# Gated FFT filter and state-space mix: x loaded by halves of its row groups, turned copies on VectorE, transform results on ScalarE

## The chip, the cores and the metric

The kernel runs on one core of one Trainium2 chip. The metric is the device time of one execution in microseconds (us), as the median of several runs. Five engines matter: TensorE (PE; its weight loads are listed apart as PEld), VectorE (DVE), ScalarE (ACT), GpSimd (POOL) and SyncE (SP), which here only issues DMA transfers. Matmul results are written to PSUM, everything else on the chip lies in SBUF, both with 128 partitions.

## The reference: what is computed

x has S = 2048 tokens of D = 1024 channels in bf16. The output mixes two branches of x by one gate per token:

```
g = sigmoid((x * gate_w).sum(-1))
a = irfft2(rfft2(x) * (w_r + 1j * w_i))            # over tokens and channels
h[t] = Lam_bar * h[t-1] + (B_bar @ x[t])           # complex, 1024 states
b = 2 * real(C @ h[t]) + x * Dskip
out = g * a + (1 - g) * b
```

The two-dimensional transform and its inverse are done as matmuls with tables of cosines and sines; the recurrence is done on VectorE with scans, between a multiplication by B on TensorE and one by C on TensorE.

## The kernel before: how it is tiled, staged and ordered

**Layout of x.** Partition p first holds the 16 tokens 16p to 16p+15, so "row" j of the text is the group of 128 tokens 16p + j. Rows 0 to 11 are loaded in natural layout into tiles called CT by SP (`load_x`, L242): one transfer for row 0, one for row 1, then five for two rows each (512 KB). TensorE then turns each of these rows, which means 8 transposes of 128x128 into one PSUM tile `pt` (`turn`, L919), and ScalarE copies the turned row into xQ, in which channels lie on partitions and tokens along the free axis (`turn_out`, L929). The source is read with a step there: order (c q g) in PSUM becomes (c, g, j, q) in xQ, so neighbouring elements of the source go to two halves g. Rows 12 to 15 come through two transposing DMA transfers (L238) into CT and are copied by ScalarE from SBUF to xQ (L925).

**The transform.** `fold` on VectorE (L943 to L954) makes sums and differences of channel halves of the turned rows: one row at a time for rows 0 to 3, two at a time for rows 4 to 15. The `fd` matmuls (L430 to L443) transform along channels into PSUM `ps_fd`; `fd_out` (L449) copies these to the tiles X, on VectorE for the groups listed in `FD_DVE` and on ScalarE for the others. The `s1` matmuls (L462) do the first step along tokens into `ps_s`; `s1_out` (L474) copies these to CT or A tiles, on VectorE for the groups listed in `S1_DVE`. SP stores them to a scratch in memory (L480), from which later stages load them.

**The recurrence.** SP loads the B matrices by 16 transposing DMA transfers (`load_B`, L259) into BT. `unit_mm` (L398) multiplies 256 columns of xQ, taken over all 16 turned rows, by BT into `psu`; so the first unit matmul needs every copy into xQ. `unit_out` (L408) copies the result to h, and VectorE multiplies by tables (`make_tab`, L281 to L307) and scans (L347 to L378). The matmuls by C (L713), the inverse transform (L594 to L671, L810) and the last matmuls (L727) follow on TensorE, and the outputs are mixed and stored.

**What sets the order.** No scheduler is at work: within one engine instructions run in program order, and the program order is written by hand. `ORDER` is a string of about 1,000 letters, one for each step of one generator: x is a step of `load_x`, T of `turn`, U of `turn_out`, f of `fold`, F of the fd matmuls and E of their copies, S of the s1 matmuls and A of their copies, G and 2 of the loads of the tables, b of `load_B`, h of `unit_mm` and H of its copies, v of the recurrence, whose pieces are numbered in `PIECES`. `SLOTS` says which of four PSUM slots each PSUM tile takes. `FILL_T` puts 22 idle transposes ahead of row 2, where TensorE would stand still otherwise. In xQ, j is a row, c a chunk of tokens, g the half and q the place in the chunk.

Of the kernel before, what the change touches and what calls it, by code (L numbers as in the profile page):

```python
# [26 lines left out]
NCH = S // TC  # L27
# [5 lines left out]
NTURN = 12  # L33
# [1 line left out]
FILL_V = (0, 0, 4)  # L35
FILL_T = {2: 22}
WARM = 7
FD_DVE = (2, 4, 6, 7)
CAST_ACT = (5, 6, 7)
ANG_ACT = (4, 5, 6, 7)  # L40
CARRY_POOL = ()
S1_DVE = (1, 4, 5)
CLOSES = (0, 1, 2, 3, 10, 4, 5, 11, 12, 6, 7, 8, 9)
PIECES = (
# [6 lines left out]
)  # L51
SLOTS = (
    "0123012310231023102310230123012031201312031203101230132031231031201312303312013213021021013010320130",
    "1220123203201320130130120321023120320321021023120312301230231201302303120",
)
MIRROR = (6, 7, 8, 9)
ORDER = (
    "xxxTVUVVVaTfVVrrUGTGG|Tfaaa|UafFffftafftUftxFEfTETUFffU22xSEkSTSTArxAfffUAUFTTEUfffUFbxwxbxbbTUEFbfE",
    "1bT~SSUfuFSFAUUUU2bbtbfAF1AtbbtrFttrbEffE11EbEh11SStbttfttttAg1~HtfufhA~tetFSSFrKHrtu1EAvfAEhtttvttt",
    "SSFtbbvvvAtEttH1Avthtftv1cttwv1tcthccctttvtcch~HFtvftHvvhuHtvfStEettStAHhtAeKrvFctcvvFhEEHKtvwtcSvtS",  # L60
    "hvvKc1vcc1vAAKKvv1c1v1hcvswcsLMvvveHHekMYsssnNHvvhHnsvvvJWWMvs3vsvNvvsssssnvssnvvs4NMvv4Njvhv553vhvv",
    "YvyJJL46H4vv5WWvhh5vvvMM78Jj7HHmn3nHvv8M44m6MnN77WW5jv+Yy5vvv3M845+mNY8nMJJMyvvv+467hvHMh5vN7N34vHmh",
    "4J8m+6n3h8v77HmH+55v4n64JMvNnMYy5vW83n+v7N474vJ568vYmmNJ7dh7NWj+v58v5vyvvd88MhvHHm8+MJm6h+n378vv7Hh8",
    "J+d4Y4YX5vv5NnJH6XXv7ny7mNNm8+hn8hvqivvvvvJvqyHihYivvyiqhivqqiYvNImvni+qJJmHIIiini+HinvdIIH+vvIIIqIN",
    "IiiiNmI+vvIInvvImvyJqii%NJINIJYJYmhvvv+vvvlylzvhHmplpzZZH+mZZZhlZvhPPRR++zyRRRlQDQHzRZZmRHZ+ZRZvoOZD",
    "QvlpDzzPovOvQBvZZlpPYvZZvBZDZRDRRRvzQDoloOBzoQOopZOoPOBlzlZRoDDZZvBZZRpQvzCvYZZvZZBZZPRDoQoo9RQQ9yRR",
    "0RRyCooD099C9Y990DD0D0Y00",
)

EVEN = ((0, 0), (2, 1), (2, 0), (0, 1))  # L70
# [72 lines left out]
def kernel(  # L143
# [17 lines left out]
    nc = tc.nc  # L161
    x = A_x[0]
# [57 lines left out]
    x_gjq = xQ.rearrange("p c d (g j q) -> p c d g j q", g=2, j=16)  # L220
# [2 lines left out]
    tab = tabp.tile([P, 4, 8, TC], BF16, name="tab")  # L223

    xn = [CT[i // 4][:, 2 * (i % 4):2 * (i % 4) + 2, :] for i in range(8)]
    x_v = x.rearrange("(p j) d -> p j d", j=16)
    x_sg = x.rearrange("(s g j) d -> g s (j d)", g=2, j=16)
    xt = CT[1][:, 4:8].rearrange("p a k -> p (a k)").rearrange("p (j d g s) -> p j d g s", j=4, d=8, g=2)
    fft = {}
# [4 lines left out]
    def load_x():  # L234
        for i in range(8):
            if i >= NTURN // 2:
                g = i - NTURN // 2
                nc.sync.dma_start_transpose(out=xt[:, :, :, g].rearrange("p j d s -> p (j d) s"), in_=x_sg[g][:, NTURN * D:])  # L238
                yield
                continue  # L240
            for js in (slice(0, 1), slice(1, 2)) if i == 0 else (slice(0, 2),):
                nc.sync.dma_start(out=xn[i][:, js], in_=x_v[:, 2 * i + js.start:2 * i + js.stop, :])  # L242
                yield

    def load_T2():
# [200 lines left out]
    def fd_out():  # L446
        for j in range(16):
            X1 = X1s[j] = gta.tile([P, 2, K], BF16, name="X1", bufs=4)
            (nc.vector.tensor_copy if j in FD_DVE else nc.scalar.copy)(  # L449
                out=X1.rearrange("p r (m e c) -> p r m e c", e=2, c=2),  # L450
# [15 lines left out]
    def s1_out():  # L466
        for j in range(16):
# [4 lines left out]
            else:  # L472
                A1 = tmp.tile([P, 2, K], BF16, name="A1_last", tag=("ang", "rot_kk", "sn_f", "cs_f")[j - 12])
            (nc.vector.tensor_copy if j in S1_DVE else nc.scalar.copy)(out=A1, in_=pss.pop(j))  # L474
            A1s[j] = A1
# [435 lines left out]
    pts = {}  # L911
# [9 lines left out]

    def turn_out():
        for j in range(16):
            if j >= NTURN:
                nc.scalar.copy(out=x_gjq[:, :, :, :, j, :].rearrange("p c d g q -> p d g c q"),  # L925
                               in_=xt[:, j - NTURN].rearrange("p d g (c q) -> p d g c q", c=NCH))
                yield
                continue
            nc.scalar.copy(out=x_gjq[:, :, :, :, j, :].rearrange("p c d g q -> p d c g q"),  # L929
                           in_=pts.pop(j).rearrange("p d (c q g) -> p d c g q", c=NCH, g=2))  # L930
            yield

    def fold():
# [228 lines left out]
    def once(f):  # L1162
# [3 lines left out]
    late_tiles = tuple(range(NEARLY))  # L1166
    acts = {
        "V": turn_vectors(), "|": turn_late_vectors(), "T": turn(), "U": turn_out(), "f": fold(), "~": mirror(), "u": fold_odd(), "F": fd(), "E": fd_out(), "S": s1(), "A": s1_out(), "1": s1_store(),
        "K": keep_A1(), "h": unit_mm(), "H": unit_out(), "t": chain(*(make_tab(jp) for jp in range(4))), "r": radii(), "a": small(),
        "g": once(gate), "e": gate_out(), "b": load_B(), "c": load_C(), "2": load_T2(), "x": load_x(), "G": load_G(), "w": load_Wcols(), "k": load_turns(),  # L1170
        "n": early_mm(), "N": early_out(), "J": early_store(), "s": middle(), "L": load_small(), "M": load_mid(), "W": load_W(),
        "3": s2(), "4": s2_out(), "j": unit_cols(), "5": times_w(), "6": is1(), "7": is1_out(), "8": is1_store(), "q": load_last(), "i": is2(), "I": is2_out(),
# [43 lines left out]
```

## Time and profile before

| what | value |
|---|---|
| median of 3 runs | 306.29 us (305.23, 306.57, 306.29) |
| span of the profiled execution, first to last instruction | 303.6 us |
| median less that span, which lies around it | 2.69 us |
| busy PE, DVE, ACT, POOL | 296.4, 289.3, 188.5, 73.3 us |
| granted TensorE clock | full in every slice |
| mean traffic with memory | 166 GB/s over the span |

The profiled execution has no time of its own beside the runs, so its span is set against the median: what lies outside the span is taken as the same before and after. A start in the timeline is in us from the start of the span; the difference of two starts on one busy engine is what one instruction really occupies, which is a little less than the duration printed for it, since instructions on VectorE and ScalarE overlap by about 0.1 us.

### The profile page before, as it was taken

Reading aid. Unit: us, or ns where it says so; the run is one execution under the profiler, and the core shown is the slowest. Engines: PE = TensorE matmul, PEld = TensorE weight load, DVE = VectorE, ACT = ScalarE, POOL = GpSimd, SP = SyncE. Lnnn points to the kernel's source line nnn. Section 1 sums busy time; section 2 is a strip of 40 time slices with the busy share of each in tenths; the row PEclk is TensorE's granted clock in tenths of the full one; section 3 lists DMA queues with packets and bytes.
Section 4 is the critical chain, followed back from the end, with each engine's and each line's share of the span. In section 5 each row is a group of like instructions: output and inputs, shape, how many; then the busy total and the mean of one; then the engine's idle time right before and its main releaser. Section 6 shows DMA issues by size and latency. Waiting matters only on the chain. (4 is left out here: it accounts for less than half of the span.)

```text
span 303.6 us, 6402 instructions
## 1 busy us (share of the span) xinstructions
PE 296.4 (98%) x2568; PEld 197.4 (65%) x2592; DVE 289.3 (95%) x340; ACT 188.5 (62%) x255; POOL 73.3 (24%) x99
## 2 busy tenths in 40 slices
PE   8999999999999999999999999999999999999995
PEld 5664677878864685458553866669657986645543
DVE  2999999999999999999999999999899999999995
ACT  4999999896532383667665865529668774343400
POOL 2100420745893001110210220202011253252330
PEclk9999999999999999999999999999999999999999
DMA  6999999989999599895948798687758876978976
GB/s 208 341 201 194 253 193 310 162 142 154 268 214 241 160 259 219 181 250 189 212 96 258 163 223 225 139 294 147 242 174 185 165 88 135 160 132 143 165 153 181
DMA packets 74157, 59.35 MB, mean 196 GB/s; under 512 B 44904, under 2 KB 61680, under 8 KB 74128
## 3 DMA queue, kind: packets, MB, share of 16 engines
q1 hardware_dynamic: 66560, 49.82, 65.8%
q0 software_dynamic: 6912, 8.69, 23.0%
q10 hardware_dynamic: 656, 0.44, 0.5%
q8 instruction: 20, 0.33, 0.4%
q14 instruction: 9, 0.07, 0.1%
HBM read 27.46 MB, written 23.08 MB: 166 GB/s over the span
## 5 line engine op out<-in xcount | busy, mean ns | idle before, releaser
L398 PE MATMUL psu<-xQ,BT 128*128 128x256 bf16 x1024 | 116.5, 273 | 0.2 <-DVE X L449 0.2
L398 PEld LDWEIGHTS <-BT 128*128 128x128 bf16 x1024 | 99.0, 98 | 17.3 <-issue 4.6
L713 PE MATMUL ps_y<-CT,h 128*128 128x512 bf16 x397 | 92.5, 379 | 0.9
L363 DVE TENSOR_TENSOR_SCAN h<-rz,h 128x2048 bf16<-128x2048 f32 (+1 forms) x20 | 70.8, 3561 | 0.0
L713 PEld LDWEIGHTS <-h 128*128 128x128 bf16 x416 | 39.6, 98 | 46.3 <-issue 2.9
L785 POOL DMA_DIRECT2D y_scratch<-su x20 | 17.3, 902 | 135.7 <-ACT su L779 105.4
L408 ACT CAST h<-psu 128x1024 bf16<-128x1024 f32 x32 | 32.3, 1011 | 18.7 <-PE psu L398 13.1
L350 DVE TENSOR_TENSOR h<-h,tab 128x4096 bf16<-128x4096 bf16 (+1 forms) x20 | 37.1, 1859 | 0.1
L744 ACT ACTIVATE ye<-ps_y,omg 128x512 f32<-128x512 f32 x26 | 17.9, 689 | 26.3 <-PE ps_y L713 11.8
L347 DVE TENSOR_TENSOR xQ<-h,tab 128x4096 bf16<-128x4096 bf16 x12 | 27.4, 2284 | 1.0 <-ACT h L408 1.0
L603 ACT CAST X<-ps_s 128x1024 bf16<-128x1024 f32 x16 | 16.2, 1010 | 14.6 <-PE ps_s L594 11.2
L727 PE MATMUL ps_q<-CT,h 128*128 128x512 bf16 (+2 forms) x110 | 21.3, 348 | 0.2
L817 ACT ACTIVATE BT<-ps_id,gB 128x1024 bf16<-128x1024 f32 x14 | 15.3, 1114 | 9.9 <-PE ps_id L810 5.7
L671 ACT CAST ZT<-ps_is 128x1024 bf16<-128x1024 f32 x16 | 15.8, 1017 | 6.2 <-PE ps_is L661 6.2
L637 ACT CAST C<-ps_is 128x1024 bf16<-128x1024 f32 x16 | 15.7, 1011 | 5.1 <-DMA xQ<-in_A_x_dram 3.4
L851 POOL DMA_DIRECT2D BT<-y_scratch x10 | 13.1, 1452 | 19.7 <-DVE BT L846 13.3
L727 PEld LDWEIGHTS <-h 128*128 128x128 bf16 x112 | 10.3, 98 | 10.4 <-DVE h L378 0.5
L779 ACT ACTIVATE su<-xs,omg 128x512 f32<-128x512 bf16 x20 | 14.2, 723 | 4.1 <-DMA y_scratch<-su 2.2
L929 ACT COPY xQ<-pt 128x1024 bf16<-128x1024 bf16 x12 | 12.2, 1082 | 1.3 <-PE pt L919 1.3
L449 ACT CAST X<-ps_fd 128x1024 bf16<-128x1024 f32 x12 | 12.3, 1062 | 1.0 <-PE ps_fd L439 0.9
L617 DVE TENSOR_TENSOR UV<-X,Wb 128x2048 bf16<-128x2048 bf16 x8 | 9.6, 1220 | 0.6 <-ACT ye L744 0.6
L617 DVE TENSOR_TENSOR UV<-X,raw 128x2048 bf16<-128x2048 bf16 x8 | 9.8, 1223 | 0.2 <-ACT X L604 0.2
(200 smaller groups left out, 397.3 us busy)
## 6 DMA issues: line engine op xcount, KB each, us to landing
y_scratch<-ye SPq DMA_DIRECT2D x20, 256.0 KB, 4.6
y_scratch<-su POOLq DMA_DIRECT2D x20, 256.0 KB, 4.7
Bb<-turn_scratch SPq DMA_DIRECT2D x16, 256.0 KB, 5.2
turn_scratch<-C SPq DMA_DIRECT2D x16, 256.0 KB, 4.1
raw<-turn_scratch SPq DMA_DIRECT2D x8, 512.0 KB, 4.3
xs<-in_A_x_dram SPq DMA_DIRECT2D x13, 256.0 KB, 3.9
out_dram<-BT SPq DMA_DIRECT2D x11, 256.0 KB, 4.3
CT<-in_A_x_dram SPq DMA_DIRECT2D x5, 512.0 KB, 6.1
```

Of the source, the lines that this page charges most:

```text
L347: nc.vector.tensor_mul(out=tmps["s"], in0=u[:, ::-1], in1=bc(i))
L350: nc.vector.tensor_mul(out=u, in0=u, in1=bc(i))
L363: nc.vector.tensor_tensor_scan(out=seg, data0=rz[:, js.start + j:js.start + j + m].rearrange("p j t -> p (j t)"), data1=seg, initial=0.0, ...
L398: nc.tensor.matmul(psu[:, j, :], lhsT=BT[4 * q + j][:, ri, d8, :], rhs=xQ[:, c, d8, :], start=(d8 == 0), stop=(d8 == 7))
L408: nc.scalar.copy(out=hs[c][:, ri, 4 * q:4 * q + 4].rearrange("p b (q j) -> p b q j", j=32), in_=psus.pop((c, q, ri)).rearrange("p b (j q) ...
L603: nc.scalar.copy(out=X2, in_=ps2s[g][b])
L617: nc.vector.tensor_mul(out=UV, in0=X2s.pop((g, b)).unsqueeze(1).to_broadcast([P, 2, 2, K]), in1=fft["Wb"][g // 2 % 2][:, :, at:at + 1, :]. ...
L671: nc.scalar.copy(out=ZT[:, 4 * kp:4 * kp + 4, :, 4 * G:4 * G + 4].rearrange("p (c r) n g -> p c r n g", c=2), in_=pszs.pop((G, kp)).rearra ...
L713: nc.tensor.matmul(psy, lhsT=hs[c][:, ri, jb, P * tq:P * (tq + 1)], rhs=CT[ri][:, jb, 512 * dh:512 * (dh + 1)], start=(i == 0), stop=(i == ...
L727: nc.tensor.matmul(psq, lhsT=hs[c][:, ri, jb, P * tq:P * (tq + 1)], rhs=CT[ri][:, jb, at:at + n], start=(i == 0), stop=(i == 15))
L744: nc.scalar.activation(out=ye, in_=psys[tb][:, K * hf:K * (hf + 1)], func=ACT.Copy, scale=omg[:, tb:tb + 1])
L785: nc.gpsimd.dma_start(out=y_dram[tb, hf], in_=xgs[tb, hf], accum_op=ALU.add)
```

## The change

x is now viewed so that partition 64g + s holds tokens 32s + 16g + j: the half g is a half of the partitions. Each step of `load_x` therefore issues two transfers of 64 partitions, 14 transfers in all where there were 7. The turned row then lies in PSUM in the order (g c q), and its copy into xQ reads and writes runs of neighbouring elements. All 16 copies of turned rows, 12 from PSUM and 4 from SBUF, go to VectorE. `FD_DVE` and `S1_DVE` are empty: the four fd copies and three s1 copies that VectorE did go to ScalarE. `PIECES`, `SLOTS` and `ORDER` are laid anew.

```diff
-FD_DVE = (2, 4, 6, 7)
+FD_DVE = ()
...
-S1_DVE = (1, 4, 5)
+S1_DVE = ()
+TURN_DVE = tuple(range(16))
...
-    "xxxTVUVVVaTfVVrrUGTGG|Tfaaa|UafFffftafftUftxFEfTETUFffU22xSEkSTSTArxAfffUAUFTTEUfffUFbxwxbxbbTUEFbfE",
+    "xTxxVG|TTUTVVVxTGfaVVfaUGVttfffTUUffbftFaFxfx|UUf2TkfErTUUFtrSxffffESFT2FfEFAafTrTawaftr2UUSFUAEExxbb",
...
-    x_v = x.rearrange("(p j) d -> p j d", j=16)
+    x_v = x.rearrange("(s g j) d -> g s j d", g=2, j=16)
...
             for js in (slice(0, 1), slice(1, 2)) if i == 0 else (slice(0, 2),):
-                nc.sync.dma_start(out=xn[i][:, js], in_=x_v[:, 2 * i + js.start:2 * i + js.stop, :])
+                for g in range(2):
+                    nc.sync.dma_start(out=xn[i][64 * g:64 * (g + 1), js], in_=x_v[g, :, 2 * i + js.start:2 * i + js.stop, :])
                 yield
...
     def turn_out():
         for j in range(16):
-            if j >= NTURN:
-                nc.scalar.copy(out=x_gjq[:, :, :, :, j, :].rearrange("p c d g q -> p d g c q"),
-                               in_=xt[:, j - NTURN].rearrange("p d g (c q) -> p d g c q", c=NCH))
-                yield
-                continue
-            nc.scalar.copy(out=x_gjq[:, :, :, :, j, :].rearrange("p c d g q -> p d c g q"),
-                           in_=pts.pop(j).rearrange("p d (c q g) -> p d c g q", c=NCH, g=2))
+            if j < NTURN:
+                src = pts.pop(j).rearrange("p d (g c q) -> p d g c q", g=2, c=NCH)
+            else:
+                src = xt[:, j - NTURN].rearrange("p d g (c q) -> p d g c q", c=NCH)
+            (nc.vector.tensor_copy if j in TURN_DVE else nc.scalar.copy)(
+                out=x_gjq[:, :, :, :, j, :].rearrange("p c d g q -> p d g c q"), in_=src)
             yield
```

From L243 on, a line of the kernel after has the number of before plus 1: the unit matmuls L399, the fd copies L450, the s1 matmuls L463 and their copies L475. `turn` is at L920, and all copies of turned rows are at L929.

VectorE before, from the last fold that needs a mirror row pair (L954) to the tables, around the time at which the last rows are folded; X and CT are the homes of the fd and s1 results:

```order
L954 TENSOR_TENSOR preT<-sums 128x2x128
L474 CAST CT_82<-ps_s_510 128x1024
L474 CAST CT_82<-ps_s_528 128x1024
L449 CAST X_592<-ps_fd 128x1024
L943 TENSOR_TENSOR preT<-xQ 128x64x2x8
L945 TENSOR_TENSOR sums<-xQ 128x64x2x8
L449 CAST X_598<-ps_fd 128x1024
```

The same place after, in which CT_83 holds the four rows that a DMA transfer has turned:

```order
L954 TENSOR_TENSOR preT<-sums 128x2x128
L929 COPY xQ<-pt 128x16x8x8
L929 COPY xQ<-CT_83 128x16x8x8 x2
L943 TENSOR_TENSOR preT<-xQ 128x64x2x8
L945 TENSOR_TENSOR sums<-xQ 128x64x2x8
L929 COPY xQ<-CT_83 128x16x8x8 x2
L303 SCALAR_TENSOR_TENSOR tab<-cs_f,cr,t_508 128x256
```

The copies of fd and s1 results have gone, and the last five copies of turned rows stand around the fold of rows 12 and 13.

SP before, from the start to the last load of x in natural layout; G_sb, raw and JP_sb are tables of constants:

```order
L242 DMA CT_82<-in_A_x_dram 128x1024 x2
L242 DMA CT_82<-in_A_x_dram 128x2048
L252 DMA G_sb<-c_G 128x1280
L252 DMA G_sb<-c_G 128x1024 x2
L242 DMA CT_82<-in_A_x_dram 128x2048
L247 DMA raw<-c_T 128x384
L247 DMA raw<-c_T 128x1152
L242 DMA CT_82<-in_A_x_dram 128x2048
L1027 DMA JP_sb<-c_JP 128x256
L242 DMA CT_83<-in_A_x_dram 128x2048
L259 DMA_TRANSPOSE BT<-in_B_B_re_dram 128x8x128
L242 DMA CT_83<-in_A_x_dram 128x2048
```

And after, with 64 partitions in each transfer of x:

```order
L243 DMA CT_82<-in_A_x_dram 64x1024 x4
L243 DMA CT_82<-in_A_x_dram 64x2048 x2
L253 DMA G_sb<-c_G 128x1280
L243 DMA CT_82<-in_A_x_dram 64x2048 x2
L253 DMA G_sb<-c_G 128x1024 x2
L260 DMA_TRANSPOSE BT<-in_B_B_re_dram 128x8x128
L243 DMA CT_82<-in_A_x_dram 64x2048 x2
L243 DMA CT_83<-in_A_x_dram 64x2048 x2
L248 DMA raw<-c_T 128x384
L1027 DMA JP_sb<-c_JP 128x256
L243 DMA CT_83<-in_A_x_dram 64x2048 x2
```

The first transposing load of B stands further ahead, the tables in raw further back, and the loads of x are 14.

TensorE before, the last rows ahead of the first unit matmul:

```order
L439 LDWEIGHTS preT
L439 MATMUL ps_fd<-G_sb,preT 128x2x128
L439 LDWEIGHTS preT
L439 MATMUL ps_fd<-G_sb,preT 128x2x128
L398 LDWEIGHTS BT
L398 MATMUL psu<-xQ,BT 128x256
```

And after, where ps_s_614 and ps_s_619 are two of the s1 results:

```order
L463 LDWEIGHTS raw
L463 MATMUL ps_s_614<-X_579,raw 128x512
...
L463 LDWEIGHTS raw
L463 MATMUL ps_s_619<-X_584,raw 128x512
L399 LDWEIGHTS BT
L399 MATMUL psu<-xQ,BT 128x256
```

Ahead of the first unit matmul now stand the s1 matmuls of 9 row groups (four matmuls of 512 columns for each), where there were 6; the three others stood behind it.

More of the change, by code (lines that the diff above doesn't have):

```diff
@@ L41 @@
 CARRY_POOL = ()
-S1_DVE = (1, 4, 5)
+S1_DVE = ()
+TURN_DVE = tuple(range(16))
 CLOSES = (0, 1, 2, 3, 10, 4, 5, 11, 12, 6, 7, 8, 9)
 PIECES = (
[6 rows of a table removed]
[5 rows of a table added]
 )
 SLOTS = (
-    "0123012310231023102310230123012031201312031203101230132031231031201312303312013213021021013010320130",
-    "1220123203201320130130120321023120320321021023120312301230231201302303120",
+    "0123012031210321032102301230123102310230213021310213201320102301230120322020310321032102132130213020",
+    "1301203120321032032031031203120312012031231231032103021302302130210320132",
 )
@@ L57 @@
 ORDER = (
-    "xxxTVUVVVaTfVVrrUGTGG|Tfaaa|UafFffftafftUftxFEfTETUFffU22xSEkSTSTArxAfffUAUFTTEUfffUFbxwxbxbbTUEFbfE",
[L59 to L67, printed above, removed]
+    "xTxxVG|TTUTVVxTGfaVVfaUGVttfffTUUffbftFaFxfx|UUf2TkfErTUUFtrSxffffESFT2FfEFAafTrTawaftr2UUSFUAEExxbb",
+    "bttff~EbbbbAuEfSSASTUFFAAEbbbEFEb1btUUfftSSSAUUhbtfff~tttAAr~tttbbKutttthFHHu1FgEESSSfFfefvtvArttvvh",
+    "1111tt~Ftth11fEttAAKuttv1111HcttttvtFhtthvvvvHEttctEtccccSSShHHetcvvvrecvcAvFthwAvttKtwvEvttt1vtrctH",
+    "SvvhvvwvhhecevAAvv1vHvvccKccvc11KKsYskHHssHvssvvvnLNMMYvvWvhHvvnnNYss3svssWJJMvMsssnsvvhMvsjvMh3Lv45",
+    "vHv4h5NNvvv644vvHWHyhJMW3vn75567mn8vW+nvM3H8JyjvmWM4545NJvM77vnvvNj44J6588+vYm+7mhMNN3vM5Yy7+hHM8844",
+    "mv6vhhv+vvHM55mWW3vHJvy77+44vmJHnn68878NJvN5Mvvm+Y75nJnvNNvv68+Yvh3hyv774m8Hvvm4y+jmhHH55vn86M77hXYJ",
+    "JN38vHnv+mYn84+v4556vNvJNJv7h+nhh8yvy78qqiivihivqiivHm+NHmvqv+JdvnvHIiimqqqvivniYIJqIHvIII+IIiIvmYvv",
+    "NNJvnvv+yIIiivmJvdIIinidIi%IIhlmNvvNvyvhzHHlXzvpllYyvZZPp+hhJmJvZZZZpPRRzRRzodHHR+mZZRPZZl+ROZQDzZvp",
+    "poRvvlPvQQQPBlvvlo+DOBXzlDZzDDZooZZRRZoZzvQQRRRpZoDDlZOOZBBOOvzBZRBoPYDZZQQvzCvvoYZZZZZZYY9RRR0QyoRR",
+    "RDDy9QCC99ooo09990DDD0000",
 )
```

11 rows, old and new, of the table PIECES are left out of this document.

## The prediction

> **What bounds the kernel now.** I read the page's span and busy times first, then the busy time by stage, cutting the span where TensorE changes its work, then TensorE's waits, and last the timelines of the engines in the first 34 us.
>
> ```profile
> span 303.6 us, 6402 instructions
> ...
> PE 296.4 (98%) x2568; PEld 197.4 (65%) x2592; DVE 289.3 (95%) x340; ACT 188.5 (62%) x255; POOL 73.3 (24%) x99
> ```
>
> ```profile
> core 0: us, PE busy (x) PEld busy (x) DVE busy (x) ACT busy (x) POOL busy (x), PEclk, DMA share, GB/s
> 0.00:5.16 5.16, 3.95 (x15) 1.84 (x16) 0.33 (x2) 1.28 (x1) 0.98 (x7) 1.00 0.62 197
> 5.16:30.33 25.17, 23.58 (x222) 15.68 (x225) 23.38 (x60) 24.59 (x33) 2.56 (x12) 1.00 1.10 244
> 30.33:286.11 255.78, 254.72 (x2254) 172.78 (x2274) 251.49 (x258) 161.51 (x221) 67.30 (x78) 1.00 0.89 192
> 286.11:300.43 14.32, 14.14 (x81) 7.07 (x79) 13.79 (x21) 1.11 (x1) 2.42 (x2) 1.00 0.86 195
> ```
>
> From 30.33, where the first unit matmul starts, to 300.43, TensorE is busy 254.72 + 14.14 = 268.86 of 270.10 us at full clock. In that stretch the list of its waits has one row, which is the very first matmul of it:
>
> ```profile
> PE psu L398 <- DVE X L449: 0.2, 1, 0.2
> ```
>
> ```profile
> 30.33 3.65 PE L398 MATMUL psu<-xQ,BT 128*128 128x256 bf16 x32 [0.19 <-DVE X L449]
> 33.91 1.04 PE L462 MATMUL ps_s<-X,raw 64*128 64x512 bf16 x8
> 34.88 0.83 PE L1001 MATMUL zps_g<-xQ,gw 128*32 128x512 bf16 x12
> ...
> 286.11 14.31 PE L727 MATMUL ps_q<-CT,h 128*128 128x512 bf16 x79
> ```
>
> So the end is the start of the first unit matmul plus a fixed amount of TensorE work. The change leaves that work alone; it can move the end only through when that stretch begins, and by waits that it brings into it. What can be won is small: in 5.16 to 30.33 TensorE stands still 25.17 − 23.58 = 1.59 us. ScalarE is the busiest there (24.59 of 25.17), VectorE follows with 23.38; both are nearly full, and the change shifts work from the one to the other.
>
> **The change part by part.** *Three s1 groups moved ahead.* Two groups occupy 34.88 − 33.91 = 0.97 us on TensorE, one 0.49. Three more of them stand ahead of the first unit matmul, so a first unit matmul at 30.33 + 1.46 = 31.79 would be no change at all. That is the mark for all that follows; these groups only change places and cost nothing.
>
> *Turned copies from ScalarE to VectorE.* All 16 must be done before the first unit matmul, so VectorE's queue up to the last of them is the path that I think sets its start.
>
> ```profile
> 6.06 0.18 DVE L1082 CAST vecF<-vps 128x24 f32<-128x24 bf16 x1 [4.91 <-PE vps L1080]
> ...
> 17.04 0.68 DVE L943 TENSOR_TENSOR preT<-xQ 128x1024 bf16<-128x1024 bf16 x1
> 17.64 0.69 DVE L945 TENSOR_TENSOR sums<-xQ 128x1024 bf16<-128x1024 bf16 x1
> ...
> 28.97 1.22 DVE L449 CAST X<-ps_fd 128x1024 bf16<-128x1024 f32 x1
> 30.10 0.68 DVE L943 TENSOR_TENSOR preT<-xQ 128x1024 bf16<-128x1024 bf16 x1
> 30.70 1.11 DVE L945 TENSOR_TENSOR sums<-xQ 128x1024 bf16<-128x1024 bf16 x1
> 31.73 1.21 DVE L449 CAST X<-ps_fd 128x1024 bf16<-128x1024 f32 x1
> ```
>
> Up to its last turned copy, VectorE's order after holds just what before has done by 31.73 (the folds of 14 rows and the small work on angles), without three L449 and three L474 and with 16 copies. One of the copies removed occupies 30.10 − 28.97 = 1.13 us, six of them 6.8. No row of before shows a copy of contiguous bf16 from PSUM on VectorE. Bounds: above, 1.13, the row of the same shape out of PSUM in f32; below, 0.60 (17.64 − 17.04), a two-operand row of 1024 bf16 elements out of SBUF. I take 0.60 for the 12 from PSUM, because the source is 16 bits wide and runs contiguously as in that row: 7.2 us, with 13.6 as the far end. For the 4 from SBUF 0.60 is the upper bound and half of it, an estimate for one operand instead of two, the lower: 1.2 to 2.4, taken at 1.8. [...]
>
> The sum: 31.73 − 6.8 + 7.2 + 1.8 = 33.9. VectorE can also begin earlier, since its first instruction now is the copy that ScalarE began at 5.27:
>
> ```profile
> 5.27 1.01 ACT L929 COPY xQ<-pt 128x1024 bf16<-128x1024 bf16 x1 [1.28 <-PE pt L919]
> ```
>
> ```profile
> core 0: us, PE busy (x) PEld busy (x) DVE busy (x) ACT busy (x) POOL busy (x), PEclk, DMA share, GB/s
> 6.06:31.73 25.67, 24.08 (x227) 16.27 (x231) 24.78 (x62) 25.19 (x36) 3.64 (x14) 1.00 1.11 244
> ```
>
> That is 6.06 − 5.27 = 0.79 earlier: 33.1. VectorE's idle time between is 25.67 − 24.78 = 0.89, of which I take half away (a queue of copies fed by TensorE has its own waits): 32.7. And the last L945 above occupies 1.03 where its twin at 17.64 takes 0.60; I let 0.3 of that go, which gives 32.4. Against the mark of 31.8 the first unit matmul is 0.6 us late. The ends: SBUF copies at 1.2, all idle and all of the 0.4 gone, 31.2 or 0.6 early by this queue; SBUF copies at 2.4, no idle gone, 33.7 or 1.9 late.
>
> *Results to ScalarE.* It loses 16 copies and gains 7.
>
> ```profile
> L449 ACT CAST X<-ps_fd 128x1024 bf16<-128x1024 f32 x12 | 12.3, 1062 | 1.0 <-PE ps_fd L439 0.9
> L929 ACT COPY xQ<-pt 128x1024 bf16<-128x1024 bf16 x12 | 12.2, 1082 | 1.3 <-PE pt L919 1.3
> ```
>
> ```profile
> 25.51 4.03 ACT L925 COPY xQ<-CT 128x1024 bf16<-128x1024 bf16 x4
> ```
>
> That is −12.2 − 4.0 + 7 × 1.06 = −8.8 us in a stretch in which it was 24.59 of 25.17 busy. It is off the path after, so this is priced at nothing; the cover is VectorE's queue. Were VectorE quicker than I think, TensorE itself would be late next, and ScalarE's relief is worth what stood idle there, 1.59 at most.
>
> *VectorE later.* In all it gains 9.0 and loses 7 × 1.13 = 7.9, so 1.1 us more in 300. In the long stretch it has 255.78 − 251.49 = 4.3 us idle, which covers this; uncovered it would cost 1.1.
>
> *14 transfers of x instead of 7, in a new order on SP.*
>
> ```profile
> 11.11 0.58 SPq L242 DMA_DIRECT2D CT<-in_A_x_dram  x1
> ```
>
> Seven more issues at up to 0.58 stand ahead of the transposing loads of B, 4 us of queue at most, less where SP waited anyway. The rows themselves have slack: the transfer of rows 10 and 11 has landed by 18.64, when a copy that needs it starts, and TensorE turns row 10 at 20.78.
>
> ```profile
> 18.64 0.24 POOL L1040 COPY Wp<-CT 128x64 bf16<-128x64 bf16 x1 [9.73 <-DMA CT<-in_A_x_dram]
> ```
>
> ```profile
> 20.78 0.61 PE L919 MATMUL pt<-ident,CT 128*128 128x128 bf16 x8
> ```
>
> So 2.1 us of delay is hidden, and I price the split at nothing; uncovered, see the first rival. For B the cover is only that the units start about 2 us later by the clock. The bounds are 0 and 2 us (4 less that 2) at the second unit group; I take 0 and keep 2 for the range.
>
> The forecast is then a span of 303.6 + 0.6 = 304.2, and with the 2.69 that lie around the span (306.29 less 303.6) 306.9 us, 0.6 above the median. A measurement of this kernel can tell about 0.5%, 1.53 us, from no change; faster therefore means below 304.76, slower above 307.82.
>
> **The rivals.**
>
> *Slower: halves of the partitions load more slowly.* Before has a place in which two transfers of 64 partitions, the halves of one Bb tile, are most of what is in flight (issued from 92.28, read at 95 to 97), and one in which x comes with 128 (10 to 13):
>
> ```profile
> 92.28 1.09 SPq L508 DMA_DIRECT2D Bb<-turn_scratch  x2
> ```
>
> ```profile
> core 0: us, PE busy (x) PEld busy (x) DVE busy (x) ACT busy (x) POOL busy (x), PEclk, DMA share, GB/s
> 10.00:13.00 3.00, 2.72 (x26) 1.89 (x26) 2.89 (x17) 3.00 (x5) 0.00 (x0) 1.00 1.05 405
> 95.00:97.00 2.00, 1.95 (x10) 0.93 (x10) 1.97 (x7) 0.25 (x1) 0.00 (x0) 1.00 1.05 232
> ```
>
> With the DMA engines as busy in both, the halves moved 232 GB/s and the full width 405. The 3.15 MB of x at these rates take 13.6 and 7.8 us: 5.8 more, so rows 10 and 11 land at 24.4 instead of 18.64, 3.6 past the turn at 20.78. Of that TensorE's 1.59 idle can absorb some: 2.0 to 3.6 late, about 309.1 us. It decides as soon as that transfer lands later than about 21. For it: the two rows. Against it: Bb's source is a scratch with shorter runs, x is read in runs of 4 KB either way, so the width may not be what makes 232. [...]
>
> *Faster: VectorE is not what is late.* If copies and waits cost less than I took, VectorE's queue ends near 31 and TensorE runs without its 1.59 us of early waits: the first unit matmul comes at 31.79 − 1.59 = 30.2, and the time is 304.4 to 304.9, say 304.7. For it: ScalarE, the fullest engine of the stage, is relieved by 8.8 us. Against: my sum for VectorE would have to fall by 2.2.
>
> *The copies do not get quicker.* If a copy from PSUM takes one element at a time whatever its order, 12 × (1.13 − 0.60) = 6.4 us come on top: first unit matmul at 38.8, 313.3 us. Then the change does not do what its contiguous order says. Against: nothing but the 16-bit source.
>
> *B late.* Transposing loads come late at the second unit group, 0 to 2 us on top of the forecast: about 308.
>
> **How the numbers follow.** Forecast 0.46 (0.40 of it within 0.5%, 0.06 slower, from the end at +1.9); halves slower 0.20; VectorE not late 0.22 (0.18 faster, 0.04 within); copies not quicker 0.05; B late 0.07 (0.04 slower, 0.03 within). So faster 0.18, same 0.47, slower 0.35. The forecast's own range is 305.7 (−0.6) to 308.2 (+1.9); the range over cases goes down to 304.3, where the gain ends, and up to 309.4, over the middle of the first rival, and leaves out the slow copies and the tail of that rival.
>
> **What the profile after would show.** Right: the first unit matmul near 32.4, ended in its wait by a VectorE copy of a turned row; a mean of about 0.65 us for the copies from PSUM; ScalarE with gaps before 30 us; still no waits of TensorE behind. Wrong: the turns of rows 4 to 11 waiting for a DMA (first rival); a first unit matmul before 31 with VectorE idle (second); copies of 1.1 us (third); waits on BT at L399 (fourth). A first unit matmul on time and yet another end would break the reading that TensorE's work alone sets what follows.

## The result, and the profile after

The changed kernel takes 313.63 us (median; 312.51 to 316.29), before 305.76 in the same comparison (305.10 to 306.57): a ratio of 1.0261, 95% interval 1.0222 to 1.0300. A second series of the changed kernel gave 1.0287 (1.0257 to 1.0317). The range of the prediction ended at 309.4. Every ratio here leaves out executions that took more than 1.5% longer than the fastest of the same kernel.

The profiled execution of after is the longest of its four (316.29 us), so the account below is of 10.9 us of span, where the medians differ by 7.9. Its page:

```profile
span 314.5 us, 6422 instructions
...
PE 298.1 (95%) x2569; PEld 198.8 (63%) x2592; DVE 293.0 (93%) x349; ACT 179.9 (57%) x246; POOL 72.2 (23%) x99
```

TensorE is busy 1.7 us more and the span is 10.9 us longer, so most of the loss is time in which it stood still. The list of its waits over the whole span, which in before had one row behind 30 us, names the places (total, times, longest):

```profile
PE aps L545 <- POOL Acol L490: 4.8, 1, 4.8
PE pt L920 <- DMA CT<-in_A_x_dram: 3.1, 2, 2.5
PE ps_s L463 <- DMA raw<-c_T: 1.7, 1, 1.7
PE psw L987 <- DVE A L982: 1.2, 1, 1.2
PE ps_s L463 <- DVE xQ L929: 0.8, 1, 0.8
...
```

TensorE's timeline puts them in time:

```profile
8.61 1.05 PE L920 MATMUL pt<-ident,CT 128*128 128x128 bf16 x16 [0.65 <-DMA CT<-in_A_x_dram]
12.15 1.05 PE L920 MATMUL pt<-ident,CT 128*128 128x128 bf16 x16 [2.48 <-DMA CT<-in_A_x_dram]
13.04 1.00 PE L434 MATMUL ps_fd<-G_sb,preT 128*128 128x256 bf16 x4
...
21.37 1.04 PE L463 MATMUL ps_s<-X,raw 64*128 64x512 bf16 x8 [1.70 <-DMA raw<-c_T]
...
37.37 3.67 PE L399 MATMUL psu<-xQ,BT 128*128 128x256 bf16 x32
...
92.17 0.29 PE L545 MATMUL aps<-ident,Acol 128*32 128x128 bf16 x1 [4.76 <-POOL Acol L490]
```

In before the same transpose came without a wait:

```profile
82.33 0.23 PE L544 MATMUL aps<-ident,Acol 128*32 128x128 bf16 x1
```

There are two places. The first unit matmul comes at 37.37, which is 37.37 − 31.79 = 5.58 us past the prediction's mark of no change. And at 92.17 a small transpose (aps, the last column of the spectrum) waited 4.76 us for GpSimd, in the stretch that had no wait before. Together they are 10.3 of the 10.9 us. Behind the second wait the granted clock is 0.50 from 92.17 to 95.02, which can hold the rest.

The first place begins with the transfers of x. Busy time by stage, before, around the time in which x arrives (last columns: granted clock, DMA share, GB/s):

```profile
8.00:12.00 4.00, 3.80 (x39) 2.68 (x37) 3.85 (x20) 3.97 (x10) 0.79 (x6) 1.00 1.05 412
```

And after:

```profile
8.00:12.00 4.00, 1.05 (x16) 0.91 (x16) 4.00 (x13) 2.04 (x5) 0.70 (x6) 1.00 1.03 241
12.00:16.00 4.00, 3.63 (x26) 2.38 (x28) 3.89 (x10) 0.22 (x1) 0.00 (x0) 0.64 1.13 257
```

The DMA engines are as busy and move 241 GB/s instead of 412. The first 640 packets of 4096 bytes in the trace are those of rows 2 to 11; their median time is 299 ns, 159 before. TensorE stands still for 2.48 us, and in the next stretch its granted clock is 0.64: the four fd matmuls at 13.04 took 1.00 us, where before has

```profile
8.92 0.60 PE L433 MATMUL ps_fd<-G_sb,preT 128*128 128x256 bf16 x4
...
11.67 1.06 PE L919 MATMUL pt<-ident,CT 128*128 128x128 bf16 x16
```

The last line is the turn of rows 4 and 5, which in before stands behind matmuls of the first rows. The new order has it right behind rows 2 and 3 (the turns at 12.15 and 8.61 in after), so these rows are needed earlier as well.

What the prediction summed for VectorE, on the other hand, came out. All forms of its copies of turned rows in after (least, median and most ns):

```profile
L929 DVE COPY xQ<-pt x12: 673/680/692, 5.3 to 33.6; 128x1024 bf16<-128x1024 bf16 x12
L929 DVE COPY xQ<-CT x4: 416/418/419, 34.2 to 36.4; 128x1024 bf16<-128x1024 bf16 x4
```

### The profile page after: what moved, and what is told of

The parts are those of the page before. It is cut to its first block, busy times and chain, and to the rows that moved or that the text cites. A ratio compares the mean times of both kernels' runs of the same rounds, so it can differ in the third digit from the quotient of the medians.

```text
span 314.5 us, 6422 instructions
## 1 busy us (share of the span) xinstructions
PE 298.1 (95%) x2569; PEld 198.8 (63%) x2592; DVE 293.0 (93%) x349; ACT 179.9 (57%) x246; POOL 72.2 (23%) x99
## 4 chain that ended last, share of the span: by engine, by line
PE 76%; DMA 13%; DVE 4%; POOL 4%; issue 1%; SPq 1%; ACT 0%; POOLq 0%; DVEq 0%; ACTq 0%
PE ps_y L714 29%; PE psu L399 26%; PE ps_q L728 7%; DMA raw<-c_T 3%; DMA Wp<-in_A_w_r_dram 3%; DMA CT<-in_A_x_dram 3%; DMA z_scratch<-zsb 3%; PE ps_is L630 3%; PE ps_is L662 2%; PE ps_id L811 2%; PE ps_s L463 2%; DMA Wp<-in_A_w_i_dram 1%; PE ps_s L595 1%; POOL Acol L490 1%; PE ps_id L807 1%
## 5 line engine op out<-in xcount | busy, mean ns | idle before, releaser
L399 PE MATMUL psu<-xQ,BT 128*128 128x256 bf16 x1024 | 115.8, 273 | 0.0
L399 PEld LDWEIGHTS <-BT 128*128 128x128 bf16 x1024 | 99.0, 98 | 17.1 <-issue 4.6
L714 PEld LDWEIGHTS <-h 128*128 128x128 bf16 x416 | 40.2, 99 | 47.7 <-issue 4.1
L450 ACT CAST X<-ps_fd 128x1024 bf16<-128x1024 f32 x16 | 15.8, 1017 | 7.0 <-PE ps_fd L444 7.0
L728 PEld LDWEIGHTS <-h 128*128 128x128 bf16 x112 | 10.4, 98 | 10.3 <-DVE h L375 0.2
L929 DVE COPY xQ<-pt 128x1024 bf16<-128x1024 bf16 x12 | 7.8, 680 | 6.2 <-PE pt L920 6.2
L463 PE MATMUL ps_s<-X,raw 64*128 64x512 bf16 x64 | 8.3, 378 | 2.5 <-DMA raw<-c_T 1.7
L920 PE MATMUL pt<-ident,CT 128*128 128x128 bf16 x96 | 7.2, 229 | 3.2 <-DMA CT<-in_A_x_dram 3.1
```

The lines of the kernel that those rows point to most:

```text
L399: nc.tensor.matmul(psu[:, j, :], lhsT=BT[4 * q + j][:, ri, d8, :], rhs=xQ[:, c, d8, :], start=(d8 == 0), stop=(d8 == 7))
L450: (nc.vector.tensor_copy if j in FD_DVE else nc.scalar.copy)(out=X1.rearrange("p r (m e c) -> p r m e c", e=2, c=2), in_=psf.pop(j).rearra ...
L714: nc.tensor.matmul(psy, lhsT=hs[c][:, ri, jb, P * tq:P * (tq + 1)], rhs=CT[ri][:, jb, 512 * dh:512 * (dh + 1)], start=(i == 0), stop=(i == ...
L728: nc.tensor.matmul(psq, lhsT=hs[c][:, ri, jb, P * tq:P * (tq + 1)], rhs=CT[ri][:, jb, at:at + n], start=(i == 0), stop=(i == 15))
```

## The experiments

The theory after the result: **A**, a transfer that fills one half of the partitions moves little more than half as many bytes a second (241 GB/s for 412 in the rows above), which starts the units late; **E**, the new order of GpSimd's queue makes the wait at 92 us. Against A stand **B** (the number of transfers, issues and completion semaphores), **C** (the new place of the tables on SP) and **D** (VectorE's fuller queue).

**Before, with x in halves.** The only edit, everything else as in before:

```diff
-                nc.sync.dma_start(out=xn[i][:, js], in_=x_v[:, 2 * i + js.start:2 * i + js.stop, :])
+                for g in range(2):
+                    nc.sync.dma_start(out=xn[i][64 * g:64 * (g + 1), js], in_=x_v[64 * g:64 * (g + 1), 2 * i + js.start:2 * i + js.stop, :])
```

> The kernel before, with only its x transfers cut into partitions 0 to 63 and 64 to 127 (order, copies and layout as before). Theory A (a transfer that fills one half of the partitions moves about 240 GB/s instead of 400): the stretch 8 to 12 us of the profile moves 230 to 250 GB/s where before moves 410, packets of 4096 bytes take near 275 ns instead of 165, the last row pair lands 3 to 5 us later, and the kernel is 2 to 4 us slower. Theory B (the number of transfers, their issues on SP and their completion semaphores cost the time): the same slowdown, but with the rate inside a transfer as before and SP idle between issues. Theory C (only the new order of the tables on SP is at fault): within 0.5 us of before.

> The kernel before with x cut into the two halves of the partitions once more, for its profile: 8 to 12 us at 230 to 290 GB/s, packets of 4096 bytes near 275 ns, TensorE waiting 3 us or more for x before the first unit matmul, which comes 3 to 6 us later than 30.3; time 311 to 314.

Measured twice: ratios to before of 1.0219 (1.0155 to 1.0284) and 1.0223 (1.0180 to 1.0267), 6.8 us, more than the 2 to 4 that were expected first. One execution of the first series took 792.96 us, for a reason that is not known, and the profile fell on it; the lines are from the second series, its stage, waits and first unit matmul:

```profile
8.00:12.00 4.00, 2.59 (x26) 1.81 (x27) 3.84 (x20) 3.97 (x9) 0.81 (x6) 1.00 1.01 303
```

```profile
PE pt L920 <- DMA CT<-in_A_x_dram: 2.5, 5, 1.0
PE psu L399 <- ACT xQ L926: 2.1, 1, 2.1
...
PE ps_fd L444 <- DMA G_sb<-c_G: 0.7, 1, 0.7
```

```profile
35.39 3.65 PE L399 MATMUL psu<-xQ,BT 128*128 128x256 bf16 x32 [2.08 <-ACT xQ L926]
```

303 GB/s is over the 290 that was expected for this stretch, but far under 412, and the packets take 275 ns in the median. With no other change the first unit matmul is 5.1 us late, by waits for x (2.5), for a table (0.7) and for the last copies of turned rows (2.1), and the span of this execution is longer by the same 5.1. So the split alone is worth most of what was lost. B and A both allow this.

**Before, with x in even and odd partitions.** As many transfers, issues and bytes:

```diff
-                    nc.sync.dma_start(out=xn[i][64 * g:64 * (g + 1), js], in_=x_v[64 * g:64 * (g + 1), 2 * i + js.start:2 * i + js.stop, :])
+                    nc.sync.dma_start(out=xn[i][g:P:2, js], in_=x_v[g:P:2, 2 * i + js.start:2 * i + js.stop, :])
```

> The kernel before, with its x transfers cut into the 64 even and the 64 odd partitions: as many transfers, issues and bytes as with halves. Theory A (which partitions a transfer reaches decides its rate; the even ones are spread over both halves): 8 to 12 us moves 380 to 420 GB/s, time within 1 us of before. Theory B (number of transfers, or 64 partitions as such): as slow as the cut into halves, 2 to 4 us.

Ratio 1.0018 (1.0000 to 1.0036). The same stage:

```profile
8.00:12.00 4.00, 3.51 (x34) 2.22 (x31) 3.84 (x20) 3.97 (x10) 0.78 (x6) 1.00 0.97 353
```

353 GB/s is less than the 380 expected, but the packets are back at 159 ns, and the time is that of before. B falls: 14 transfers of 64 partitions cost next to nothing here (0.2%), if these are spread over the whole width. It is which partitions a transfer fills (275 ns a packet for halves, 159 for these). The memory side is ruled out as well: each of these transfers reads the same tokens (32s + 16g + j for all s) as one of after, which puts them into the partitions 64g + s.

**After, with one transfer in the changed layout.** The memory side walks the two halves:

```diff
-                for g in range(2):
-                    nc.sync.dma_start(out=xn[i][64 * g:64 * (g + 1), js], in_=x_v[g, :, 2 * i + js.start:2 * i + js.stop, :])
+                nc.sync.dma_start(out=xn[i][:, js], in_=x_v[:, :, 2 * i + js.start:2 * i + js.stop, :])
```

> The changed kernel with each x step as one transfer of 128 partitions again, in the changed layout (the memory side walks the halves, the same rows land in the same places); all else as changed. Theory A: 8 to 12 us moves about 400 GB/s, TensorE no longer waits for x before rows 2 and 4 (3.1 us) nor for the table raw (1.7 us), the first unit matmul comes at 31.5 to 33.5 instead of 37.4, the time falls by 4 to 6 us. Theory C (the order on SP): the wait for raw stays, the time falls by under 2. The wait for Acol at 87 us is a matter of its own and may stay.

This decides nothing between A and C. The ratio is 1.1616 (1.1551 to 1.1681), because such a transfer is far slower than either:

```profile
8.00:12.00 4.00, 1.88 (x17) 1.39 (x17) 1.35 (x4) 0.21 (x1) 0.32 (x2) 0.50 0.16 54
```

54 GB/s at a DMA share of 0.16, with packets of the usual 162 ns: as a mean 0.16 × 16 = 2.6 of the 16 engines worked. It says nothing on the half transfers.

**After, with x loaded as before.** Layout and transfers of before, so VectorE reads the turned rows in steps of two elements:

```diff
-                src = pts.pop(j).rearrange("p d (g c q) -> p d g c q", g=2, c=NCH)
+                src = pts.pop(j).rearrange("p d (c q g) -> p d g c q", g=2, c=NCH)
```

> The changed kernel with x loaded as before (128 partitions, 16 neighbouring tokens to a partition) and so with VectorE reading the turned rows out of PSUM in steps of two elements; order and engines as changed. Theory A: rate and first unit matmul as with the single transfer in the changed layout, 4 to 6 us faster than changed, if the stepped copies cost the same 0.60 us; if they take one element per step of the clock, 1.1 us each and 12 x 0.5 = 6 us of VectorE more, which would eat the gain: no faster than changed.

Ratio 1.0307 (1.0270 to 1.0343): the second of the two expectations. The copies' row:

```profile
L928 DVE COPY xQ<-pt x12: 1206/1212/1224, 5.3 to 34.4; 128x1024 bf16<-128x1024 bf16 x12
```

A stepped copy takes 1.21 us, a contiguous one 0.68. Twelve of them add 12 × 0.53 = 6.4 us to VectorE's queue. TensorE's list has no wait for x or raw here, but waits for these copies (1.3 and 2.2 us are the largest sums), so the gain at the transfers is eaten. The changed layout does what it is for; what it pays for it is the transfer.

**After, with transfers of 128 partitions and contiguous copies.** TensorE can deliver the halves: a turn is a matmul by the unit matrix, and with its columns permuted the turned row comes out in the order (g s), so that VectorE copies it contiguously (0.68 us in the profile of this run). The loads are those of before.

```diff
+    ident_t = cpool.tile([P, P], BF16, name="ident_t")
+    nc.gpsimd.tensor_copy(out=ident_t.rearrange("p (g s) -> p g s", g=2), in_=ident.rearrange("p (s g) -> p g s", g=2))
...
-                nc.tensor.transpose(out=pt[:, i, :], in_=xn[j // 2][:, j % 2, P * i:P * (i + 1)], identity=ident)
+                nc.tensor.transpose(out=pt[:, i, :], in_=xn[j // 2][:, j % 2, P * i:P * (i + 1)], identity=ident_t)
```

> The changed kernel with x loaded as before, 128 partitions to a transfer; the turned rows still lie contiguously by halves, since TensorE turns them with a permuted unit matrix (one extra copy of 128x128 on GpSimd at the start). Copies, engines and order as changed. Theory A (the half transfers set the late start): x arrives at the rate of before, copies stay at 0.68 us, VectorE's queue ends its last turned copy at 32 to 33, the first unit matmul comes there instead of 37.4, and the time falls by 4 to 5 us to 308 to 310, with the wait for Acol left. Theory D (the new order or the fuller VectorE sets the start): under 2 us faster.

Ratio 1.0079 (1.0035 to 1.0123), so 1.8 to 2.1% of the 2.6 to 2.9% are gone with the half transfers. Its ten executions fall into two groups, three of 305.5 to 306.9 us and seven of 308.9 to 311.0; the median of all ten, 309.64, is 1.4% above before, which would make it 1.3 to 1.5%. The contiguous turned rows, the copies on VectorE and the order of SP are all still there, so C and D fall as causes of more than the remaining 0.8 to 1.4%. From the profile, of an execution of 310.96 us:

```profile
PE aps L546 <- POOL Acol L491: 2.5, 1, 2.5
PE vps L1098 <- DMA vec<-in_B_Dskip_dram: 1.4, 1, 1.4
```

```profile
34.12 3.67 PE L400 MATMUL psu<-xQ,BT 128*128 128x256 bf16 x32
```

The waits for x and raw are gone and the wait for Acol still stands. The first unit matmul comes 3.3 us earlier than in after, but behind the 32 to 33 that were expected. A wait of 1.4 us for a small vector (Dskip), which the list of after does not have, stands ahead of it, and TensorE's granted clock behind that wait is 0.57 (8 to 12).

**After, with GpSimd's queue laid otherwise.** Five letters of ORDER are moved, so that the last copies into Acol stand ahead of the steps on the columns of W (the rows of GpSimd, of after and of this kernel):

```diff
-COPY Acol<-A_last 128x2
+COPY Acol<-A_last 128x2 x2
 DMA Wp<-in_A_w_i_dram 128x15x2
...
+COPY Acol<-A_last 128x2 x2
 COPY Wc<-Wp 128x2x16
...
 CAST omg<-omg_bf 128x16
-COPY Acol<-A_last 128x2 x3
```

> The changed kernel with its x in halves, and only GpSimd's queue laid otherwise: the four last small copies to Acol stand right behind the results that they read, ahead of the steps that wait for the columns of W. Theory E (TensorE's wait of 4.8 us at 87 us is the order of GpSimd's queue): that wait falls under 1 us and the time falls by 2 to 4.5 us. Rival: the results or the columns of W are late anyway, the same wait moves to the matmuls on Wc just ahead, and the time falls by under 1.

Ratio 1.0178 (1.0143 to 1.0213): 0.8 to 1.1% less, 2.5 to 3.3 us, and no wait for Acol in its list. E holds. Why, GpSimd's timeline shows; in before

```profile
75.94 2.25 POOL L489 COPY Acol<-A_last 128x2 bf16<-128x2 bf16 x2 [3.81 <-ACT A_last L474]
78.12 0.28 POOL L1054 COPY Wc<-Wp 128x32 bf16<-128x32 bf16 x1
```

and in after

```profile
83.42 1.36 POOL L1054 COPY Wc<-Wp 128x32 bf16<-128x32 bf16 x1 [3.20 <-DMA Wp<-in_A_w_i_dram]
...
88.06 4.05 POOL L490 COPY Acol<-A_last 128x2 bf16<-128x2 bf16 x3
```

The small copies stood behind six others that waited for a transfer until 83.42, and they run to 92.1, where aps starts. Part of the wait has changed place in this kernel's own profile: `Wrev_ps` waits 1.0 us for Wc and `Zrev_ps` 2.8 us for Zp, in an execution of 318.2 us; the three others took 309.95 to 311.9.

**Both edits together.**

> Both edits: x in transfers of 128 partitions with a permuted unit matrix, and the small copies ahead on GpSimd. If the two places are all there is, the start costs 0 to 1 us against before and the wait is gone: 304.5 to 307.5, the sum of the two gains. If they hide each other (the wait at 87 us is set by chains that do not move with TensorE's start, so an earlier start makes the wait longer), 307.5 to 311.

Ratio 1.0011 (0.9981 to 1.0041): the loss is accounted for, with one part for each edit. Seven of its ten executions took 305.1 to 305.7 us; the three others took 308.8 to 310.3, longer than any of before in the same series (304.6 to 307.0). From the DVE and PE timelines of its profile, which is of one of the three (309.84 us):

```profile
31.62 0.75 DVE L930 COPY xQ<-CT 128x1024 bf16<-128x1024 bf16 x2
```

```profile
32.96 3.67 PE L400 MATMUL psu<-xQ,BT 128*128 128x256 bf16 x32
...
82.93 0.23 PE L546 MATMUL aps<-ident,Acol 128*32 128x128 bf16 x1
...
100.38 0.16 PE L527 MATMUL Zrev_ps<-Zp,JP_sb 128*128 128x2 bf16 x1 [2.41 <-DVE Zp L559]
```

The last turned copy ends at 32.4 and the first unit matmul comes at 33.0, without a wait: TensorE's own matmuls run up to it. The wait of 2.41 us further on has no counterpart in before; whether it is what makes the three executions longer is not shown.

**Halves on two queues.** The changed kernel with the second half of each step issued by ScalarE:

```diff
-                    nc.sync.dma_start(out=xn[i][64 * g:64 * (g + 1), js], in_=x_v[g, :, 2 * i + js.start:2 * i + js.stop, :])
+                    (nc.scalar if g else nc.sync).dma_start(out=xn[i][64 * g:64 * (g + 1), js], in_=x_v[g, :, 2 * i + js.start:2 * i + js.stop, :])
```

> The changed kernel with the second half of each x step issued on ScalarE's queue instead of SP's, so that transfers to both halves of the partitions are in flight at the same time. [...] If halves as such are slow however they are issued: 230 to 290 GB/s and 312 to 315.

Ratio 1.0421 (1.0389 to 1.0453), 318.33 us in the median and so worse than the 312 to 315 of the expectation, and inconclusive on the transfers: ScalarE's queue held back its issues for rows 6 to 9 to 12.77, where SP had issued its halves of them at 8.75, and ScalarE's own work stood behind these issues.

```profile
12.77 3.54 ACTq L243 DMA_DIRECT2D CT<-in_A_x_dram  x2
16.36 0.17 ACT L1099 CAST vecF<-vps 128x8 f32<-128x8 bf16 x1 [3.92 <-DMA CT<-in_A_x_dram]
```

TensorE waited 3.4 us for the copy behind those issues, and 3.0 us for row 0. The packets took 286 ns in the median and 8 to 12 us moved 237 GB/s, but the two halves of a step were often not issued together, so whether two halves at once run at the full rate stays open.

**The changed kernel once more.**

> The changed kernel itself once more, nothing edited, for a second profile: 312 to 315 us. Theory: the late start (first unit matmul near 37) is in every execution, since the order of the transfers is fixed; the waits between 80 and 105 us, whose chain runs over GpSimd's slow transfers, differ from one execution to the next and make the spread of 312 to 316.

313.87 to 314.98 us, ratio 1.0287. Its first unit matmul comes at 37.13, as late as in the other profile; the wait for Acol is 2.5 us instead of 4.8.

**Two attempts at a gain.** To both edits was added first the fill of the radii on GpSimd ahead of the loads of W, then TensorE's late turn of the vectors as in before:

```diff
-KKtwvEvttt1vtrct
+KKtrwvEvttt1vtct
...
-xTxxVG|TTUTV
+xTxxVGTTUT|V
```

> As the kernel with both edits (x in 128 partitions with a permuted unit matrix, small copies ahead on GpSimd), and one fill of the radii on GpSimd (rz, two instructions) moved ahead of the loads of the columns of W, behind which VectorE's scan waited 2.5 to 2.7 us. If that wait feeds the chain to TensorE's later waits: 1 us faster in the mean, 304 to 305.5. If VectorE's wait is covered: 305.6 as without.

> As the one with the radii moved, and TensorE's two turns of the vectors Dskip and gate_w put behind the turn of row 3 as in the kernel before, since they waited 1.3 us for their small transfers there. If that wait is on the path: first unit matmul 0.5 to 1.3 us earlier and the time 303.5 to 305, faster than before by up to 0.5%. If VectorE's queue of copies binds anyway: no change to the one with the radii alone.

Ratios 1.0036 (1.0015 to 1.0057; one execution of 443.81 us is left out) and 1.0013 (0.9996 to 1.0030). VectorE's wait for rz is gone in both, TensorE's for the vectors in the second, and neither beats the kernel with both edits or before: the one wait was covered, and behind the other the copies of turned rows were due next (a wait of 1.8 us for DVE xQ stands in the list of the second).

## Why the prediction was wrong

**What held.** The reading that TensorE sets the end, and that the change acts through the first unit matmul and through waits behind it: 5.6 us at the one, 4.8 at the other. The price of the copies: 0.60 us from start to start out of PSUM as taken, 0.33 out of SBUF, near the lower bound. The sum for VectorE gave a first unit matmul at 32.4; in the four profiles with the transfers repaired it comes at 33.0, 33.4, 34.1 and 35.2, and with both edits the time is within 0.4% of before, under the forecast of 306.9. One small term was off: the forecast added 2.69 us for what lies around the span, taken from the median and the span of another execution, and in every execution on record the time is 1.7 to 1.9 us above its own span.

**The step that failed first**: "I price the split at nothing", since 2.1 us of delay were hidden at rows 10 and 11. The split takes rate away from the first row on (3 to 5 us moved 200 GB/s in after and 327 in before), and rows 2 and 4, which TensorE needs at once in the new order, have no slack: the 0.65 and 2.48 us are waits for these. The slack was read at the last rows alone. In place of nothing, the split alone made the first unit matmul 5.1 us late in before, and without it that matmul of the changed kernel comes 2.1 to 4.4 us earlier than 37.37 in the four profiles named above. The first rival had this mechanism, and its two rows (232 and 405 GB/s) measured 241 and 412 here, but it got a chance of 0.20, because another reason could be thought of for the 232. And in after its price of 2.0 to 3.6 us was too low by two terms. One is the clock: the stand of 2.48 us was followed by 3.4 us at half the clock, an estimated 1.5 us, since TensorE was busy for 3.2 of these 3.4 (1.00 for 0.60 in the matmuls above). The other is what is queued behind x: the first part of the table raw, issued at 12.03 instead of 4.98, and the s1 matmuls waited for raw until 21.3, for 1.70 us. On SP before

```profile
4.98 2.09 SPq L247 DMA_DIRECT2D raw<-c_T  x2
```

and after

```profile
12.03 0.35 SPq L248 DMA_DIRECT2D raw<-c_T  x1
```

About half of that delay is the new order on SP: with full transfers in the same order raw is issued at 8.63 (the kernel with the permuted unit matrix alone), and there TensorE does not wait for it. In before with halves neither term appears (clock 1.00, no wait for raw); other waits take their place.

**The step that failed second**: "The change leaves that work alone", said of everything behind the first unit matmul. The orders of VectorE, TensorE and SP were compared, and not that of GpSimd, which is 24% busy. There the small copies had moved behind steps that wait for a transfer. Worth 2.5 to 3.3 us, and no term of the prediction.

**A warning in the numbers.** The rival of the copies that do not get quicker gave 313.3, and 313.63 was measured. Its mechanism is refuted by the row of 0.68 us. A time that fits is no proof.

**The rate and the clock.** From 8 to 12 us, at DMA shares of 0.97 to 1.05, the traffic was 412 GB/s with x by the full width, 241 (after) and 303 (before) with x by halves, in stretches in which tables of the full width moved as well, and 353 with x by even and odd partitions. Packets of 4096 bytes took 159 ns at full width and by even and odd partitions, and 275 to 299 by halves. So in these runs the rate followed which partitions a transfer fills; why a half is slower is not shown. Half the clock followed stands of 2.48 us (after) and 1.43 us (the permuted matrix alone), and did not follow one of 2.08 us (before with halves); what decides it is not shown.

## What to carry to other kernels

Ask of a transfer which partitions it fills: in the kernel before a cut into halves cost 2.2% of the time (packets of 275 ns for 159), a cut into even and odd ones 0.2% (159), and where the halves are wanted in the free axis after a turn, a permuted unit matrix gave them without touching the load, with copies of 0.68 us. Price a slower stream at the first consumer that has no slack, with what is queued behind it and with the clock that a standing TensorE can lose (here half, for 3.4 us after a stand of 2.48). And when an order is laid anew, compare every queue to its end, the idlest engine's too: a copy of two columns, put behind a step that waits, held TensorE for 4.8 us.

## What the runs showed of the hardware that I had not expected

- Packets of 4096 bytes into SBUF took 159 ns in the median when a transfer filled all partitions or every second one, and 275 to 299 ns when it filled one half, at DMA shares of 0.97 to 1.05 from 8 to 12 us.
- One transfer of 128 partitions whose memory side leads with a dimension of two ran at 54 GB/s and a DMA share of 0.16.
- After TensorE had waited 2.48 us its clock was granted at half for 3.4 us. In the profile of the kernel with both edits a wait of 2.41 us at 100 us was followed by 16 matmuls of 512 columns in 5.30 us, where 16 of them had taken 3.63 at 83 us. The length of a stand alone did not decide in these runs: half the clock also followed one of 1.43 us in the profile with the permuted unit matrix alone (a mean of 0.57 from 8 to 12 us), and not one of 1.29 us in that with both edits (1.00 from 8 to 12) or one of 2.08 us in before with halves (32 unit matmuls in 3.65 us behind it, as in before).
